# Two small products in a gated attention and SwiGLU kernel: full-array matmuls replaced by 32-wide tiles of the TensorE array

## Chip, cores and metric

The kernel runs on one NeuronCore of a Trainium2 chip. The metric is device time in microseconds for one execution. The profile is of one execution; its engines are PE (TensorE, matmul), PEld (TensorE, weight loads), DVE (VectorE), ACT (ScalarE), POOL (GpSimd) and SP (SyncE, which issues the DMAs here).

## What is computed

A token block x (2048 x 512, bf16) goes through two branches, which a gate mixes. Branch A is linear attention with 32 heads of 16 features; branch B is a SwiGLU block with 1376 hidden features.

```python
g = sigmoid((x * gate_w).sum(-1, keepdims=True))
# A: H = 32 heads, Dh = 16
q, k, v = split(x @ wqkv)
phi = lambda t: where(t > 0, t + 1, exp(t)) + 1e-6
pq, pk = phi(q), phi(k)
kv = einsum("bhsd,bhse->bhde", pk, v)
z = einsum("bhsd->bhd", pk)
num = einsum("bhqd,bhde->bhqe", pq, kv)
den = einsum("bhqd,bhd->bhq", pq, z)[..., None] + 1e-6
a = reshape(num / den) @ wo
# B
b = (silu(x @ w1) * (x @ w3)) @ w2
out = g * a + (1 - g) * b
```

## The kernel before

The 512 features are four chunks of 128 (`KC = 4`), the tokens sixteen tiles of 128 (`NT = 16`) or four blocks of 512 (`NTB = 4`). Weights and x stay in SBUF for the whole run. The order of the work on each engine is the order of the program text (a manual schedule); a tile waits where its operands or its buffer are not ready. All DMAs are issued from SP's queue, in order.

1. *Projections.* For each token tile q and k are projected (L169), phi is applied on ACT and DVE (L182 to L187), POOL adds up pk (L201), and G = xT pk is accumulated over all tiles in banks 0 to 3 (`g_step`, L217). So kv is never formed from v: it is wvT G, taken later.
2. *The first token block of branch B, with the small products between.* `glu_step` (L264, L270) runs ten times for each token block; each time it is 4 + 4 matmuls of 128x128 against 512 columns into banks 4 to 7, a Silu on ACT (L275) and a product on DVE into hT (L276). The ten steps cover the full chunks of hidden features; the rest of 96 features goes through `rem_step` (L231), which also makes the gate. After step 2 comes `kv_step`: for each of four chunks c, four matmuls accumulate a 128x128 block (8 heads x 8 heads of 16), and DVE multiplies it by the mask `bmask`, which keeps the eight 16x16 diagonal blocks (L408). After step 4 comes `m2_step`: M2[c] = kvT[c].T @ wo[c], one matmul of 512 columns for each chunk (L417), copied out by ACT (L419) and DVE (L421) in turns. After that the denominators: POOL multiplies pq by z (`den_products`, L283), DVE sums by head and takes the reciprocal (L287 to L294), POOL scales pq by it into pqs (`den_scale`, L298), and SP issues a DMA transpose of pqs into pqT (L303).
3. *Outputs.* `out_step` multiplies pqT by M2 (L429, four matmuls) and hT by w2 (L442, eleven matmuls), ACT scales the first with the gate (L434), DVE adds the second (L446), SP stores the tile. The other three token blocks then go through `glu_step` and `out_step` in the same way, each output step carrying the denominators of a tile of the next block.

PSUM has eight banks: 4 to 7 turn over for projections and GLU steps (`mm_tile`), 0 to 3 hold G and later turn over for kv, M2 and the outputs (`ab_tile`).

The masks are built on POOL at the start (L73 to L78), ahead of the memsets of `hrem` (L84). In kv's blocks and in kvT the rows are features of v, the columns features of k; in M2 the rows are features of q in their natural order, since pqT's chunk c holds features 128c to 128c + 127.

Of the kernel before, what the change touches and what calls it, by code (L numbers as in the profile page):

```python
# [8 lines left out]
ACT = mybir.ActivationFunctionType  # L9
ALU = mybir.AluOpType  # L10
AX = mybir.AxisListType
FP32 = mybir.dt.float32
BF16 = mybir.dt.bfloat16
# [3 lines left out]
def kernel(  # L17
# [17 lines left out]
    nc = tc.nc  # L35
    P = nc.NUM_PARTITIONS
# [3 lines left out]
    H = 32  # L40
    Dh = D // H
    KC = D // P
# [7 lines left out]
    HPC = P // Dh  # L50
    ZP = 4
    NR = 2 * FR + 1

    x2d = A_x.flatten_outer_dims()
    out2d = out.flatten_outer_dims()
# [5 lines left out]
    consts = ctx.enter_context(tc.tile_pool(name="consts", bufs=1))  # L61
# [10 lines left out]
    bmask = consts.tile([P, HPC, Dh], BF16, name="bmask")  # L72
    nc.gpsimd.memset(bmask[:], 1.0)  # L73
    nc.gpsimd.affine_select(
        out=bmask[:], in_=bmask[:], pattern=[[-Dh, HPC], [0, Dh]], compare_op=ALU.is_ge,
# [3 lines left out]
        out=bmask[:], in_=bmask[:], pattern=[[Dh, HPC], [0, Dh]], compare_op=ALU.is_ge,  # L79
        fill=0.0, base=Dh - 1, channel_multiplier=-1,  # L80
    )
    hrem = [consts.tile([P, TPB, P], BF16, name=f"hrem{i}") for i in range(2)]
    for h in hrem:
        nc.gpsimd.memset(h[:], 0.0)  # L84
# [16 lines left out]
    wv = consts.tile([P, KC, D], BF16, name="wv")  # L101
    wo = consts.tile([P, KC, D], BF16, name="wo")
# [29 lines left out]
    with nc.allow_non_contiguous_dma(reason="gate column"):  # L132
        dq.dma_start(
            out=wr[:, :, 2 * FR : NR], in_=gate_w.rearrange("(kc d o) -> d kc o", d=P, o=1)
        )
# [11 lines left out]
    pq = consts.tile([P, NT, D], BF16, name="pq")  # L147
    pqT = consts.tile([P, KC, S], BF16, name="pqT")
    Gsb = consts.tile([P, KC, D], BF16, name="Gsb")
    kvT = consts.tile([P, KC, P], BF16, name="kvT")  # L150
    M2 = consts.tile([P, KC, D], BF16, name="M2")
    g_all = consts.tile([P, NT], FP32, name="g_all")
    omg_all = consts.tile([P, NT], FP32, name="omg_all")
# [9 lines left out]
    def ab_tile():  # L163
        turn["ab"] += 1
        return bank[(turn["ab"] - 1) % 4]
# [57 lines left out]
    def rem_step(tb):  # L223

        hr = hrem[tb % 2]
        for half in range(2):
            ps = mm_tile()[:].rearrange("p (j n) -> p j n", j=2)
            for j in range(2):
                t = tb * TPB + half * 2 + j
                for kc in range(KC):  # L230
                    nc.tensor.matmul(  # L231
                        ps[:, j, 0:NR], lhsT=xT[:, kc, t * P : (t + 1) * P],
                        rhs=wr[:, kc, 0:NR], start=(kc == 0), stop=(kc == KC - 1),
                    )
# [44 lines left out]
    rden = {}  # L279
# [16 lines left out]
    def den_scale(t):  # L296
        pqs = work.tile([P, D], BF16, tag="pqs", bufs=3, name="pqs")
        nc.gpsimd.tensor_tensor(  # L298
            out=pqs[:].rearrange("p (h d) -> p h d", d=Dh),
            in0=pq[:, t, :].rearrange("p (h d) -> p h d", d=Dh),  # L300
            in1=rden[t][:, :, None].to_broadcast([P, H, Dh]), op=ALU.mult,
        )
        dq.dma_start(out=pqT[:, :, t * P : (t + 1) * P], in_=pqs[:], transpose=True)  # L303

    def den_step(t):

        den_sums(t)
        if t + 1 < NT:
            den_products(t + 1)
        den_scale(t)  # L310
# [86 lines left out]
            nc.scalar.activation(out=Gsb[:, kc, :], in_=bank[kc][:], func=ACT.Copy)  # L397

    def kv_step():
        kv_ps = ab_tile()[:].rearrange("p (c q) -> p c q", q=P)  # L400
        for c in range(KC):
            cs = slice(c * P, (c + 1) * P)
            for kc in range(KC):
                nc.tensor.matmul(  # L404
                    kv_ps[:, c, :], lhsT=wv[:, kc, cs], rhs=Gsb[:, kc, cs],
                    start=(kc == 0), stop=(kc == KC - 1),
                )
        nc.vector.tensor_tensor(  # L408
            out=kvT[:], in0=kv_ps,
            in1=bmask[:].rearrange("p h d -> p (h d)")[:, None, :].to_broadcast([P, KC, P]),  # L410
            op=ALU.mult,
        )

    def m2_step():
        for c in range(KC):
            ps = ab_tile()
            nc.tensor.matmul(ps[:], lhsT=kvT[:, c, :], rhs=wo[:, c, :], start=True, stop=True)  # L417
            if c % 2 == 0:
                nc.scalar.activation(out=M2[:, c, :], in_=ps[:], func=ACT.Copy)  # L419
            else:  # L420
                nc.vector.tensor_copy(out=M2[:, c, :], in_=ps[:])  # L421

    def out_step(tb, tt):
        t = tb * TPB + tt
# [38 lines left out]
    for tb in range(NTB):  # L463
        for fc in range(FC):
            glu_step(tb, fc)
            if tb == 0:
                if fc in den_at:
                    den_step(den_at[fc])
                if fc == 2:
                    kv_step()  # L470
                if fc == 4:
                    m2_step()
                    z_order()
                    den_products(0)
                if fc == 7:
                    rem_step(0)
        for tt in range(TPB):
            out_step(tb, tt)
            if tb + 1 < NTB:
                if tt == 0:  # L480
                    hT[tb + 1] = work.tile([P, FC + 1, TB], BF16, tag="hT", name="hT")
                if tt == 1:
                    rem_step(tb + 1)
                den_step((tb + 1) * TPB + tt)
# [30 lines left out]
```

## Time and profile before

| | us |
|---|---|
| Median of 3 runs (179.22 to 179.92) | 179.44 |
| Span of the profiled execution | 177.9 |
| TensorE busy in it | 174.3 |
| Four GLU matmuls of 512 columns (L264 or L270), each time | 0.86 |
| kv, 16 matmuls of 128 columns (L404) | 0.89 |
| M2, 4 matmuls of 512 columns (L417) | 0.86 |
| Mask product on DVE (L408) | 0.69 |
| M2's copies: ACT each, DVE each | 0.59, 0.68 |
| pqs product on POOL (L298), each of 16 | 1.06 |

The table's step times are pieces of the chain of work that ended last: the profile follows the end of the kernel back, at each step to what released it. In the lines of groups, the form "128*128 128x512" is the weight block and the moving block; the three durations after a colon are the shortest, the median and the longest in ns. Ends of matmuls are modelled, so the recorded length of one (379 ns for 512 columns) is longer than the distance between two starts (216 ns). The granted clock of TensorE is 1.000 over the whole span.

### The profile page before, as it was taken

How to read it: one execution, taken by the hardware profiler on the slowest of the kernel's cores; microseconds unless marked ns; L12 is line 12 of the kernel's file. 1: busy time of each engine (PE TensorE's matmuls, PEld its weight loads, DVE VectorE, ACT ScalarE, POOL GpSimd, SP SyncE). 2: the span in 40 equal slices, each digit the busy share in tenths (PEclk: the TensorE clock that was granted, in tenths of full speed). 3: DMA queues.
4: the chain of work that ended last, by engine and by line, in shares of the span. 5: the costliest groups of instructions: out<-in, count | busy, mean ns of one | idle time of the engine just before them, and what ended most of it. 6: DMA issues, size and time to landing. Idle time of an engine off the chain costs nothing.

```text
span 177.9 us, 2504 instructions
## 1 busy us (share of the span) xinstructions
PE 174.3 (98%) x879; PEld 84.1 (47%) x879; DVE 101.5 (57%) x195; ACT 62.2 (35%) x113; POOL 63.5 (36%) x105
## 2 busy tenths in 40 slices
PE   8999999999999999999999999999999999999993
PEld 5444444444454464644444464444445444444453
DVE  0299798888865888666344166634325564333222
ACT  3255444544744332331333223242321223342130
POOL 5077667557301676846300044540004432000000
DMA  6978959993103025243100013520000342000001
GB/s 175 266 209 233 168 100 315 391 350 111 33 0 29 0 55 66 66 95 106 29 0 4 0 33 85 94 57 4 0 0 29 88 92 59 0 0 0 29 33 59
DMA packets 29724, 15.41 MB, mean 87 GB/s; under 512 B 21552, under 2 KB 28048, under 8 KB 29712
## 3 DMA queue, kind: packets, MB, share of 16 engines
q1 hardware_dynamic: 29440, 15.25, 35.2%
q8 instruction: 7, 0.11, 0.3%
q10 hardware_dynamic: 272, 0.01, 0.1%
q14 instruction: 5, 0.04, 0.1%
HBM read 8.56 MB, written 2.10 MB: 60 GB/s over the span
## 4 chain that ended last, share of the span: by engine, by line
PE 98%; DVE 0%; issue 0%
PE bank L442 21%; PE bank L264 19%; PE bank L270 19%; PE bank L169 16%; PE bank L429 8%; PE bank L217 8%; PE bank L231 3%; PE bank L317 2%; PE bank L323 1%; PE bank L404 1%; PE bank L417 0%; DVE o L446 0%
## 5 line engine op out<-in xcount | busy, mean ns | idle before, releaser
L276 DVE TENSOR_TENSOR hT<-bank,sg 128x512 bf16<-128x512 f32 x40 | 27.3, 682 | 32.4 <-PE bank L270 32.4
L264 PE MATMUL bank<-xT,w 128*128 128x512 bf16 x160 | 41.1, 379 | 0.0
L270 PE MATMUL bank<-xT,w 128*128 128x512 bf16 x160 | 41.1, 379 | 0.0
L442 PE MATMUL bank<-w,hT 128*128 128x512 bf16 (+3 forms) x198 | 40.7, 355 | 0.0
L275 ACT ACTIVATE sg<-bank 128x512 bf16<-128x512 f32 x40 | 23.9, 597 | 46.7 <-PE bank L264 46.7
L298 POOL TENSOR_TENSOR pqs<-pq,rden 128x512 bf16<-128x512 bf16 x16 | 16.9, 1056 | 55.7 <-issue 48.2
L169 PE MATMUL bank<-wqk,xT 128*128 128x512 bf16 x128 | 31.2, 386 | 0.0
L442 PEld LDWEIGHTS <-hT 128*128 128x128 bf16 (+1 forms) x198 | 18.5, 98 | 19.8
L446 DVE SCALAR_TENSOR_TENSOR o<-bank,omg_all,aga 128x512 bf16<-128x512 f32 (+2 forms) x18 | 12.4, 692 | 25.6 <-PE bank L442 25.5
L201 POOL TENSOR_TENSOR zacc<-zacc,pk 128x128 f32<-128x128 f32 x56 | 23.3, 446 | 10.4 <-DVE pk L187 10.4
L270 PEld LDWEIGHTS <-w 128*128 128x128 bf16 x160 | 15.7, 98 | 18.9
L264 PEld LDWEIGHTS <-w 128*128 128x128 bf16 x160 | 15.6, 98 | 18.4
L434 ACT ACTIVATE aga<-bank,g_all 128x512 f32<-128x512 f32 x16 | 11.0, 688 | 28.9 <-PE bank L429 28.9
L169 PEld LDWEIGHTS <-xT 128*128 128x128 bf16 x128 | 12.6, 99 | 15.1 <-issue 0.6
L283 POOL TENSOR_TENSOR pr<-pq,zb 128x512 f32<-128x512 bf16 x16 | 18.5, 1156 | 0.1
L217 PE MATMUL bank<-pk,xN 128*128 128x512 bf16 x64 | 16.4, 379 | 0.0
L429 PE MATMUL bank<-M,pqT 128*128 128x512 bf16 x64 | 16.4, 378 | 0.0
L182 ACT ACTIVATE eq<-bank 128x512 bf16<-128x512 f32 x16 | 9.4, 598 | 16.0 <-PE bank L169 16.0
L187 DVE SCALAR_TENSOR_TENSOR pk<-bank,emk 128x512 bf16<-128x512 f32 x16 | 11.1, 692 | 1.6
L182 ACT ACTIVATE ek<-bank 128x512 bf16<-128x512 f32 x16 | 9.5, 597 | 7.1 <-PE bank L169 7.1
L187 DVE SCALAR_TENSOR_TENSOR pq<-bank,emq 128x512 bf16<-128x512 f32 x16 | 11.1, 692 | 0.5
L287 DVE TENSOR_REDUCE den<-pr 128x32 f32<-128x512 f32 x16 | 10.8, 676 | 0.0
(48 smaller groups left out, 82.6 us busy)
## 6 DMA issues: line engine op xcount, KB each, us to landing
w<-in_B_w_dram SPq DMA_DIRECT2D x3, 1280.0 KB, 10.1
out_dram<-o SPq DMA_DIRECT2D x15, 128.0 KB, 1.9
wqk<-in_A_wqkv_dram SPq DMA_DIRECT2D x4, 256.0 KB, 3.9
xN<-in_A_x_dram SPq DMA_DIRECT2D x1, 1024.0 KB, 5.8
xN<-in_A_x_dram SPq DMA_DIRECT2D x2, 256.0 KB, 3.1
xN<-in_A_x_dram SPq DMA_DIRECT2D x1, 512.0 KB, 3.7
wv<-in_A_wqkv_dram SPq DMA_DIRECT2D x1, 512.0 KB, 11.0
wo<-in_A_wo_dram SPq DMA_DIRECT2D x1, 512.0 KB, 12.0
```

The lines of the kernel that those rows point to most:

```text
L169: nc.tensor.matmul(ps[:], lhsT=xT[:, kc, t * P : (t + 1) * P], rhs=w[:, kc, :], start=(kc == 0), stop=(kc == KC - 1),)
L182: nc.scalar.activation(out=e[:], in_=ps[:], func=ACT.Exp)
L187: nc.vector.scalar_tensor_tensor(out=dst, in0=ps[:], scalar=0.0, in1=em[:], op0=ALU.max, op1=ALU.add)
L201: nc.gpsimd.tensor_tensor(out=(zaccb if t == NT - 1 else zacc)[:, cs], in0=zacc[:, cs], in1=pk[t][:, cs], op=ALU.add,)
L217: nc.tensor.matmul(bank[kc][:], lhsT=xN[:, t, kc * P : (kc + 1) * P], rhs=pk[t][:], start=(t == 0), stop=(t == NT - 1),)
L264: nc.tensor.matmul(g_ps[:], lhsT=w1[:, kc, fs], rhs=xT[:, kc, tok], start=(kc == 0), stop=(kc == KC - 1),)
L270: nc.tensor.matmul(u_ps[:], lhsT=w3[:, kc, fs], rhs=xT[:, kc, tok], start=(kc == 0), stop=(kc == KC - 1),)
L275: nc.scalar.activation(out=sg[:], in_=g_ps[:], func=ACT.Silu)
L276: nc.vector.tensor_tensor(out=hT[tb][:, fc, :], in0=u_ps[:], in1=sg[:], op=ALU.mult)
L283: nc.gpsimd.tensor_tensor(out=pr[t][:], in0=pq[:, t, :], in1=zb[:], op=ALU.mult)
L429: nc.tensor.matmul(a_ps[:], lhsT=pqT[:, c, ts], rhs=M2[:, c, :], start=(c == 0), stop=(c == KC - 1),)
L442: nc.tensor.matmul(b_ps[:, 0:w], lhsT=hT[tb][:n, fc, tl], rhs=w2[:n, fc, cs], start=(fc == 0), stop=(fc == FC),)
```

## The change

The heads need 16x16 diagonal blocks, and two heads fit in a 32x32 block, so all of kv lies in sixteen 32x32 diagonal blocks. The change computes only these, and uses the array in parts.

*The mask.* `bm32` (128x32) is made from `bmask` by adding its four column groups, three additions on POOL.

*kv.* For each chunk c and each contraction chunk kc, four matmuls, one for each group g of 32 features: 32 columns of weights from wv against 32 columns of G, written to partitions 32g to 32g + 31. There are 64 matmuls of 32 columns in place of 16 of 128, and the result is 128 x (4 x 32).

*M2.* For each c and g one matmul with 32 rows of kvT as weights (rows 32g on, 32 columns) against the same 32 rows of wo (512 columns), written to partitions 32c on of bank g: sixteen matmuls of 512 columns, each with a row group and a column group of its own, in place of four. The four copies then run by g, after all sixteen matmuls in program order.

*pqs.* M2's rows now come in the order g, c, head, feature, so the product that writes pqs permutes its output in the same way. The number of instructions and the DMA transposes stay the same.

```diff
+    RP = 32
+    RB = P // RP
+    HPR = RP // Dh
...
+    bm32 = consts.tile([P, RP], BF16, name="bm32")
+    bm_g = bmask[:].rearrange("p (g h) d -> p g (h d)", g=RB)
+    nc.gpsimd.tensor_tensor(out=bm32[:], in0=bm_g[:, 0, :], in1=bm_g[:, 1, :], op=ALU.add)
+    for g in range(2, RB):
+        nc.gpsimd.tensor_tensor(out=bm32[:], in0=bm32[:], in1=bm_g[:, g, :], op=ALU.add)
...
-    kvT = consts.tile([P, KC, P], BF16, name="kvT")
+    kvT = consts.tile([P, KC, RP], BF16, name="kvT")
...
-            out=pqs[:].rearrange("p (h d) -> p h d", d=Dh),
-            in0=pq[:, t, :].rearrange("p (h d) -> p h d", d=Dh),
-            in1=rden[t][:, :, None].to_broadcast([P, H, Dh]), op=ALU.mult,
+            out=pqs[:].rearrange("p (g c h d) -> p c g h d", c=KC, h=HPR, d=Dh),
+            in0=pq[:, t, :].rearrange("p (c g h d) -> p c g h d", c=KC, h=HPR, d=Dh),
+            in1=rden[t][:].rearrange("p (c g h) -> p c g h", c=KC, h=HPR)[
+                :, :, :, :, None
+            ].to_broadcast([P, KC, RB, HPR, Dh]),
+            op=ALU.mult,
...
-        kv_ps = ab_tile()[:].rearrange("p (c q) -> p c q", q=P)
+        kv_ps = ab_tile()[:, 0 : KC * RP].rearrange("p (c q) -> p c q", q=RP)
         for c in range(KC):
-            cs = slice(c * P, (c + 1) * P)
             for kc in range(KC):
-                nc.tensor.matmul(
-                    kv_ps[:, c, :], lhsT=wv[:, kc, cs], rhs=Gsb[:, kc, cs],
-                    start=(kc == 0), stop=(kc == KC - 1),
-                )
+                for g in range(RB):
+                    fs = slice(c * P + g * RP, c * P + (g + 1) * RP)
+                    nc.tensor.matmul(
+                        kv_ps[g * RP : (g + 1) * RP, c, :], lhsT=wv[:, kc, fs],
+                        rhs=Gsb[:, kc, fs], start=(kc == 0), stop=(kc == KC - 1),
+                    )
         nc.vector.tensor_tensor(
             out=kvT[:], in0=kv_ps,
-            in1=bmask[:].rearrange("p h d -> p (h d)")[:, None, :].to_broadcast([P, KC, P]),
+            in1=bm32[:, None, :].to_broadcast([P, KC, RP]),
             op=ALU.mult,
         )
...
     def m2_step():
+        ps = [ab_tile() for _ in range(RB)]
         for c in range(KC):
-            ps = ab_tile()
-            nc.tensor.matmul(ps[:], lhsT=kvT[:, c, :], rhs=wo[:, c, :], start=True, stop=True)
-            if c % 2 == 0:
-                nc.scalar.activation(out=M2[:, c, :], in_=ps[:], func=ACT.Copy)
+            for g in range(RB):
+                rows = slice(g * RP, (g + 1) * RP)
+                nc.tensor.matmul(
+                    ps[g][c * RP : (c + 1) * RP, :], lhsT=kvT[rows, c, :], rhs=wo[rows, c, :],
+                    start=True, stop=True,
+                )
+        for g in range(RB):
+            if g % 2 == 0:
+                nc.scalar.activation(out=M2[:, g, :], in_=ps[g][:], func=ACT.Copy)
             else:
-                nc.vector.tensor_copy(out=M2[:, c, :], in_=ps[:])
+                nc.vector.tensor_copy(out=M2[:, g, :], in_=ps[g][:])
```

## The prediction

> **What bounds the kernel now.** I read the page from the top: busy times, then the chain that ended last, then the lines of TensorE that the change touches, then what stands near them on the other engines.
>
> ```profile
> span 177.9 us, 2504 instructions
> PE 174.3 (98%) x879; PEld 84.1 (47%) x879; DVE 101.5 (57%) x195; ACT 62.2 (35%) x113; POOL 63.5 (36%) x105
> ...
> PE 98%; DVE 0%; issue 0%
> ```
>
> TensorE is busy for 98% of the span, and the chain is TensorE's for 98% too: after the start nothing holds it up, so a nanosecond added to its stream or taken from it is one at the end. The execution's span is 177.9 us and the median of the runs is 179.44; the 1.5 us between lie around the span, and I add my difference to the median.
>
> The chain in order of time, around the two steps that change:
>
> ```profile
> 51.36 0.86 PE bank L270 x4
> 52.23 0.89 PE bank L404 x16
> 53.12 0.86 PE bank L264 x4
> ...
> 55.71 0.86 PE bank L270 x4
> 56.57 0.86 PE bank L417 x4
> 57.44 0.86 PE bank L264 x4
> ```
>
> kv (L404) takes 0.89 us for 16 matmuls of 128 columns, 55.6 ns each; M2 (L417) takes 0.86 us for 4 of 512 columns, 216 ns each. Both sit in a dense stream. Together they are 1.75 us, 1% of the span: all that this change could win is less than that, while what it may lose has no such roof.
>
> The lines by themselves show what the rates hide:
>
> ```profile
> L404 PEld LDWEIGHTS <-wv x16: 97/98/98, 51.9 to 52.8; 128*128 128x128 bf16 x16
> L404 PE MATMUL bank<-Gsb,wv x16: 219/219/219, 52.1 to 52.9; 128*128 128x128 bf16 x16
> ...
> L417 PEld LDWEIGHTS <-kvT x4: 98/98/98, 56.2 to 56.8; 128*128 128x128 bf16 x4
> L417 PE MATMUL bank<-wo,kvT x4: 379/379/379, 56.4 to 57.1; 128*128 128x512 bf16 x4
> ```
>
> Each matmul has a weight load of its own. One takes 98 ns and starts about one matmul ahead (0.2 us ahead of a 512-column neighbour). A matmul of 128 columns is recorded as 219 ns though the next starts 55.6 ns on, one of 512 as 379 against 216: some 163 ns is depth of pipeline that a dense stream hides.
>
> **The change on TensorE.** Three terms.
>
> *kv.* 16 loads and 16 matmuls become 64 loads of 32 columns and 64 matmuls of 32 columns, on four column groups. A quarter of the columns, four times the instructions: without any overlap between groups the streamed columns are the same 2048, with perfect overlap a quarter. The trace has no matmul this short. Bounds per load and matmul: the two rates above lie on a line, (216 - 55.6)/(512 - 128) = 0.418 ns a column and 2.2 ns fixed, which gives 15.6 ns at 32 columns; and the nearest measured pair, the 128-column one, needs 55.6 ns, which is also what 32 columns would need if load and issue don't shrink with the columns. Perfect overlap of four groups lies below both, at 16 x 15.6 = 0.25 us in all. I take the middle of 15.6 and 55.6, 35 ns: a load of a quarter of the columns should be shorter, but the fixed part of a load is paid 64 times and is hidden behind a matmul that is now a quarter as long. 64 x 35 = 2.24 us against 0.89: **+1.35 us** (bounds -0.64 and 64 x 55.6 - 890 = +2.67).
>
> [...]
>
> *M2.* 4 matmuls of 512 columns become 16 of 512 columns, each on a 32x32 block of the array, with 16 loads. If the blocks run side by side, the step lasts 15 starts and one stream: 15 x 35 + 216 = 0.74 us against 0.86, **-0.12 us**. Bounds: all sixteen in the time of one, 0.22 us, -0.65; starts at 55.6 ns, 1.05 us, +0.19; and, with no concurrency at all, 16 x 216 = 3.46, +2.6, which I treat as a rival.
>
> *Going from one division of the array to another.* The stream goes full array, four column groups, full array, sixteen blocks, full array: four transitions, and the trace of before has none. Each costs between nothing and the pipeline's depth of 163 ns, if the next matmul must wait for the last to leave. I take half, 80 ns: 4 x 80 = **+0.33 us** (bounds 0 and +0.65).
>
> [...]
>
> Sum: 1.35 - 0.12 + 0.33 = **+1.56 us**: 177.9 becomes 179.5 in the profile, and 179.44 becomes **181.0**.
>
> **The change elsewhere.** All of it I cost at nothing; this is the cover.
>
> *The mask product* (L408): 128 elements a row where there were 512. It takes 0.69 us; 128x192 from a bank takes 0.36 (L241), so some 0.35 us of VectorE is saved. VectorE idles about 1.1 us ahead of each hT product there, and kvT was ready at 53.9 for a use at 56.4. Nothing gained; and if kv ends 1.4 us later, kvT is still done well ahead, since the two GLU steps between move with it.
>
> *The 32-column mask*: three additions of 128x32 on POOL, each between 0.1 us (the small memsets) and 0.45 (128x128 f32, L201), 0.3 to 1.3 us together. POOL has idle time of 6.5 us just after, before the first zacc. Without it zacc would start later by as much.
>
> *The M2 copies*: still two of 0.6 us on ScalarE and two of 0.68 on VectorE. All four banks fill at nearly the same time, so the first copy starts up to 0.5 us later, and M2 is wanted at 67.2, eight microseconds after. If they pushed sg and hT of the next GLU step, TensorE would not see it before a bank is wanted again, a step on (1.73 us).
>
> *The pqs product* (L298) writes its 512 elements permuted, in runs of 32, sixteen times:
>
> ```profile
> L298 POOL TENSOR_TENSOR pqs<-pq,rden 128x512 bf16<-128x512 bf16 x16 | 16.9, 1056 | 55.7 <-issue 48.2
> ...
> 56.88 0.65 POOL L388 COPY zb<-zpk 128x512 bf16<-128x512 bf16 x1 [10.03 <-DMA zpk<-zrow]
> ...
> 62.32 3.86 SPq L303 DMA_TRANSPOSE pqT<-pqs  x2
> 66.27 1.22 SPq L254 DMA_TRANSPOSE hT<-hrem  x1
> ```
>
> A permuted operand is seen in zb: 0.65 us for 512 elements read with a step, 0.61 for zacc's plain cast of 512 (L197). So +0.03 us or nothing an instruction; the upper bound, a doubling, is a rival below. The transposes that follow read pqs as before: the same bytes and issues, and SP's queue is moved past nothing.
>
> **The rivals.**
>
> *A, the tiles overlap as meant.* Starts at 15.6 ns: kv 64 x 15.6 = 1.0 us (+0.11), M2 15 x 15.6 + 216 = 0.45 (-0.41), transitions 0 to +0.65: between -0.3 and +0.35, so **179.1 to 179.8**, which can't be told from no change. For it: the straight line through the two rates, and that loads and matmuls overlap now. Against: that line was measured from 128 columns up. It decides as long as a pair comes in under some 27 ns in both steps, since 64 x 27 - 890 + 15 x 27 + 216 - 860 + 330 = +0.9 us: up to 180.3. [...] Chance 0.27.
>
> *B, a real gain*: kv overlaps fourfold (0.25 us, -0.64) and M2 takes one matmul's time (-0.65) with transitions almost free: **178.2 to 178.5**. It needs every bound at its best. Chance 0.05.
>
> *C, short pairs cost as much as long ones.* The supply of instructions, not the array, sets the pace: kv +2.67, M2 +0.19, transitions +0.65, sum +3.5, **182.9**. For it: 128 instructions come where 32 did, and the burst of 16 pairs at 55.6 ns may have been queued ahead during the 216 ns matmuls before it, so it proves no lasting rate. Chance 0.19. [...]
>
> *D, the blocks don't run together*, so the change doesn't do what it says: M2 3.46 us (+2.6), kv +2.67, transitions +0.65: **185.4**. Nothing in the trace speaks for serial blocks but that it shows no two matmuls on one array. Chance 0.07 with what lies between C and D.
>
> *E, POOL becomes late.* At three times its 1.06 us the first pqs ends at 64.4 in place of 62.3, the next pr product (1.16) at 65.6, the second pqs at 68.8. SP serves in order: that tile's transpose issues until 70.0, and the hT transpose behind it goes from 66.3 to 70.1 and lands 2.4 us later, at 72.5. The last of the eleven matmuls of the first output tile wants it at 68.27 + 10 x 0.216 = 70.4: 2.1 us of stall, **181.5** from this alone. At twice its time the same sum gives 70.3 and no stall, so it decides from about there, and a later TensorE adds slack. Against it stands zb's row. Chance 0.02.
>
> **How the numbers follow.** Forecast (+0.9 to +2.4 us) 0.40, A 0.27, B 0.05, C 0.19, D 0.07, E 0.02. About 0.5%, 0.9 us, is what a measurement of this kernel can tell from no change. Faster is B, 0.05; same is A, 0.27; slower is the rest, 0.68. The likeliest is the forecast, 181.0. The range leaves out B, D and the best edge of A: 179.1 to 183.6, its top being C with 0.7 us on it for the transitions' loads (a load of 98 ns that can't be hidden, four times 0.1, and as much again for M2's).
>
> **What would show it.** The chain's piece for kv: 64 matmuls in 2.2 us means 35 ns a pair; 1.0 is A, 3.6 is C. M2's piece of 0.7 us from first start to the next GLU step; 0.3 is B, 3.5 is D. Gaps of TensorE at the four borders of up to 0.16 us. pqs at 1.06 to 1.1 us, kvT near 0.3, no new wait of TensorE on POOL, VectorE or DMA. The prediction is wrong if kv's piece is under 1.5 us or over 3.3, or if TensorE stands still anywhere else.

## The result: 178.53 us, a little faster

The changed kernel takes 178.53 us (median of 19 runs, 178.17 to 179.16) against 179.23 us for the kernel before in the same comparison. The ratio is 0.9961, 95% interval 0.9951 to 0.9971: 0.70 us less, with 0.52 to 0.88 by the interval. The forecast was 181.0 us, range 179.1 to 183.6; the time lies below the range and on the other side of no change. (The forecast adds its difference to 179.44, the median of the three runs known then; over all 19 runs the kernel before takes 0.2 us less.)

The page of the changed kernel, busy times and the chain:

```profile
span 177.4 us, 2610 instructions
PE 172.9 (97%) x922; PEld 83.5 (47%) x939; DVE 101.0 (57%) x195; ACT 62.1 (35%) x113; POOL 64.2 (36%) x108
...
PE 97%; issue 1%; DVE 0%
```

TensorE is still the bound. (The matmul count is 922 where the loads are 939: some matmul records are missing, and the chain shows such holes as 0.05 us of "issue".) The chain in order of time around the two steps, in us from the start of the span, then length:

```profile
51.42 0.86 PE bank L278 x4
52.28 0.59 PE bank L416 x64
52.87 0.32 PE bank L272
...
55.57 0.86 PE bank L278 x4
56.43 0.36 PE bank L431 x16
56.80 0.97 PE bank L272 x4
```

L416 is kv, L431 M2, L272 and L278 the gate and up matmuls. kv's piece is 0.59 us where it was 0.89, M2's 0.36 where it was 0.86. What follows each is longer: the first full matmul after a step takes 0.32 in place of 0.22, and the four after M2 take 0.97 in place of 0.86. Both have to be counted, and the starts of the matmuls do that best. From the last full matmul before a step to the second or third one after it, less 216 ns for each full matmul in between and the first, kv takes **0.70 us** (0.89 before) and M2 **0.47 us** (0.86 before): -0.20 and -0.39.

The rest of the trace is as forecast: the mask product is short, pqs isn't slower, and TensorE waits for nobody. The views are of the tiles kvT and pqs:

```profile
L420 DVE TENSOR_TENSOR kvT<-bank,bm x1: 280/280/280, 53.0 to 53.0; 128x128 bf16<-128x128 f32 x1
...
L306 POOL TENSOR_TENSOR pqs<-pq,rden x16: 1055/1056/1060, 60.7 to 146.5; 128x512 bf16<-128x512 bf16 x16
```

The starts of single matmuls, from the trace's records, show where the time went (ns from one start to the next; "full" is a 512-column matmul on the whole array):

```
kv   full to first 309 | 3 4 3 28 | 5 2 4 15 | 4 2 4 15 ...
     behind the 33rd: 8 9 8 8 11 8 9 8 8 ...        last to full 116
M2   full to first 309 | 3 4 3 3 4 3 3 4 3 3 ...    last to full 317, then 226
```

In kv four matmuls start within some 10 ns, and after the first four each next four come 25 ns later; behind the 33rd there is one every 8.3 ns. M2's sixteen all start within 50 ns. A full matmul holds the next one off for 216 ns, so 309 means 93 ns lost on the way into the tiles. Theory T, put to the test below: the tiles of a step do overlap, and each step that leaves the full array costs some 0.2 us for leaving and coming back.

### The profile page after: what moved, and what is told of

Its sections match the earlier page's. It is cut to its first block, busy times and chain, and to the rows that moved or that the text cites. A ratio compares the mean times of both kernels' runs of the same rounds, so it can differ in the third digit from the quotient of the medians.

```text
span 177.4 us, 2610 instructions
## 1 busy us (share of the span) xinstructions
PE 172.9 (97%) x922; PEld 83.5 (47%) x939; DVE 101.0 (57%) x195; ACT 62.1 (35%) x113; POOL 64.2 (36%) x108
## 4 chain that ended last, share of the span: by engine, by line
PE 97%; issue 1%; DVE 0%
PE bank L460 21%; PE bank L278 20%; PE bank L272 19%; PE bank L177 16%; PE bank L225 8%; PE bank L447 8%; PE bank L239 3%; PE bank L328 2%; PE bank L334 1%; PE bank L416 0%; PE bank L431 0%; DVE o L464 0%
## 5 line engine op out<-in xcount | busy, mean ns | idle before, releaser
L278 PE MATMUL bank<-xT,w 128*128 128x512 bf16 x158 | 40.8, 379 | 0.2
L272 PE MATMUL bank<-xT,w 128*128 128x512 bf16 x156 | 40.5, 379 | 0.2
L278 PEld LDWEIGHTS <-w 128*128 128x128 bf16 x160 | 15.6, 98 | 18.9
L272 PEld LDWEIGHTS <-w 128*128 128x128 bf16 x160 | 15.5, 98 | 18.5 <-issue 0.2
```

The costliest lines, as they stand in the source:

```text
L272: nc.tensor.matmul(g_ps[:], lhsT=w1[:, kc, fs], rhs=xT[:, kc, tok], start=(kc == 0), stop=(kc == KC - 1),)
L278: nc.tensor.matmul(u_ps[:], lhsT=w3[:, kc, fs], rhs=xT[:, kc, tok], start=(kc == 0), stop=(kc == KC - 1),)
```

## The experiments

**Each half alone.** m2_alone keeps the new M2 and the old kv matmuls; kv's mask product then takes the diagonal blocks in four small products. kv_alone keeps the new kv and the old M2, with kvT zeroed at the start.

```diff
 # m2_alone: kv_step's product, after the old 16 matmuls
...
+        for g in range(RB):
+            rows = slice(g * RP, (g + 1) * RP)
+            nc.vector.tensor_tensor(out=kvT[rows, :, :], in0=kv_ps[rows, :, rows],
+                in1=bm32[rows, None, :].to_broadcast([RP, KC, RP]), op=ALU.mult)
 # kv_alone: the same, from the new 64 matmuls into a zeroed kvT of 128 columns a chunk
...
+                out=kvT[rows, :, rows], in0=kv_ps[rows, :, :],
...
```

Expected of m2_alone:

> Theory T (from the two traces): the tiles of a step overlap, and each step that leaves the full array costs some 0.09 us going in and 0.11 coming out. M2 alone then keeps its gain of 0.39 us: the step takes 0.47 us between full-array matmuls against 0.86, and kv stays at 0.89; the ratio to before is about 0.9978. Rival R3: the gain comes from other parts (kv's product on VectorE, the smaller kvT), and M2 alone gives nothing: 1.000.

Expected of kv_alone:

> T: kv alone gains 0.20 us (0.70 us between full-array matmuls against 0.89), M2 stays at 0.86; ratio to before about 0.999, and the gains of kv_alone and m2_alone add up to the change's 0.6 to 0.7 us. R3: all of the rest of the gain, some 0.3 us, is here or in neither. The record's term of +1.35 us would give 1.0075.

Measured: m2_alone 178.83 us, ratio 0.9962 (0.9949 to 0.9976); kv_alone 179.34 us, ratio 0.9989 (0.9976 to 1.0003). kv_alone's interval includes no change, so its gain rests on the trace. The steps in the traces keep their lengths. The chain of m2_alone:

```profile
51.75 0.89 PE bank L415 x16
...
56.10 0.36 PE bank L431 x16
56.46 0.97 PE bank L272 x4
```

From the last full matmul before kv to the last matmul of the kernel it is 123.06 us before, 122.67 in m2_alone (-0.39), 122.87 in kv_alone (-0.19) and 122.47 in the changed kernel (-0.59): the halves add up. By the runs' times m2_alone won more, 0.68 us with 0.43 to 0.92 by the interval, than the 0.39 of its step in the trace.

**Everything but the matmuls.** products_only is the kernel before with the 32-column mask on POOL and kv's product as four small ones into a zeroed kvT.

```diff
...
+            nc.vector.tensor_tensor(
+                out=kvT[rows, :, rows], in0=kv_ps[rows, :, rows],
+                in1=bm32[rows, None, :].to_broadcast([RP, KC, RP]), op=ALU.mult)
...
```

Expected:

> The kernel before with everything around the matmuls that m2_alone has: the 32-column mask on POOL and kv's product as four small ones, here into a zeroed kvT; all matmuls as before. m2_alone measured 0.68 us less than before while its step in the trace is only 0.39 us shorter. [...] Rival R3: the parts around the matmuls are worth some 0.2 to 0.3 us, 0.9985.

Measured: 179.38 us, ratio 0.9993 (0.9976 to 1.0010); kv is 0.89 and M2 0.86 in its chain, and from the last full matmul before kv to the last matmul it is 123.06 us, as in the kernel before: behind that point the parts around the matmuls are worth nothing. The interval of the runs does not shut out 0.2 us, so the small remainder of m2_alone stays open; the likeliest cause, not shown, is scatter ahead of the change. The last full matmul before kv starts at 51.85 us in the profile of before and at 51.37 in that of m2_alone, with the same matmuls up to there.

**Do the column groups overlap, or are short matmuls cheap by themselves?** kv_one_group issues the same 64 matmuls with the group outermost.

```diff
-        for c in range(KC):
-            for kc in range(KC):
-                for g in range(RB):
+        for g in range(RB):
+            for c in range(KC):
+                for kc in range(KC):
```

Expected:

> The same 64 matmuls in the order group, chunk, contraction, so that 16 in a row use one column group. T: neighbours can no longer overlap, a pair costs at least the straight line's 15.6 ns and up to the 55.6 of a 128-column pair: kv's first to last start takes 1.0 to 3.5 us in place of 0.47, the kernel is 0.5 to 3.0 us slower than the changed one. Rival R1: short pairs are cheap by themselves, at 6 to 8 ns each, with no overlap needed: 0.47 us and no difference.

Measured: 179.59 us, ratio 1.0012 (0.9998 to 1.0025), some 0.9 us over the changed kernel. Its chain:

```profile
51.75 1.46 PE bank L416 x64
53.20 0.32 PE bank L272
```

kv's piece goes from 0.59 to 1.46 us, by the order of its instructions alone. Between two starts in one group lie 25 ns, matmul after matmul, whether or not the next one adds to the same block; only where one group ends and the next begins do two streams interleave. So a load and matmul of 32 columns take 25 ns in a column group, and four groups share those 25 ns when their turns alternate: 6.25 ns a pair. R1 falls.

**What sets the 8.3 ns?** kv_thrice does kv's 64 matmuls three times over.

```diff
-        for c in range(KC):
+        for c in [c for _ in range(3) for c in range(KC)]:
```

Expected:

> kv's 64 matmuls done three times over, 192 in a row. T with a supply limit: the first 32 or so come four in 25 ns from a queue filled ahead, all later ones 8.3 ns apart, pairs 65 to 96 too: 0.2 + 160 x 8.3 = 1.5 us from first to last start, +1.1 us on the changed kernel. Rival: 8.3 ns belongs to the later chunks (columns or bank), so the 6.25 ns pattern returns at matmuls 65 and 129: 1.4 us. The record's 35 ns a pair: 6.7 us.

Measured: 179.94 us, ratio 1.0029 (1.0013 to 1.0046), +1.2 us on the changed kernel; the piece in the chain, which counts 189 of the 192 matmuls, is

```profile
52.39 1.66 PE bank L416 x189
54.05 0.97 PE bank L272 x4
```

The pattern of four in 25 ns ends after the 33rd start and never comes back: all the others are 8.3 ns apart, and 128 more pairs x 8.3 = 1.07 us is what the piece grew by (1.66 - 0.59). So 8.3 ns isn't bound to a place in the bank; it behaves like the rate at which new pairs are supplied once a stock of some 33 pairs is used up. That there is a stock is the author's reading and was not seen directly; m2_thrice, below, shows that, if there is one, it is not refilled all the time.

**Do M2's blocks run at the same time?** m2_thrice does its sixteen matmuls three times.

```diff
-        for c in range(KC):
+        for c in [c for _ in range(3) for c in range(KC)]:
             for g in range(RB):
```

Expected:

> M2's sixteen matmuls done three times over. T: sixteen blocks run at once, the next pass waits only for the stream of its own block: +2 x 216 ns, +0.43 us on the changed kernel, with starts in clusters of sixteen 216 ns apart. Rival R4, the block matmuls are spread over time and only their starts are close (the recorded ends are modelled): 2 x 16 x some part of 216 ns, up to +6.9 us.

Measured: 179.45 us, ratio 0.9999 (0.9980 to 1.0019), +0.7 us on the changed kernel with some 0.4 either way. The piece in the chain:

```profile
56.32 0.85 PE bank L431 x48
57.17 0.97 PE bank L272 x4
```

It grew by 0.49 us (0.85 - 0.36) for 32 more matmuls, where 0.43 was expected. The starts come in three clusters of sixteen, whose first members are 227 and 216 ns apart; behind the seventh of the last cluster they are 8.3 ns apart in place of 3.3, which is the rest. From the last full matmul before M2 to the last matmul of the kernel the trace is longer by the same 0.49 us (118.81 against 118.32). All sixteen blocks together take the time of one stream of 512 columns; R4 falls.

This run also bounds what can be said of the stock. Sixteen matmuls every 220 ns use a pair every 13.8 ns on average, so a stock of 33 that gained one pair every 8.3 ns all along would never run out here. But here too the weight loads pause behind the 33rd and then come 8.3 ns apart. The 34th load starts 416 ns after the first matmul of the step, which is recorded as 385 ns long; in kv_thrice it is 220 ns and 190. In both it comes some 30 ns after the recorded (modelled) end of that first matmul. So it looks as if nothing new is supplied until the step's first matmul has ended; no run was made to test this.

**What does a change of tiling cost?** kv_spread puts kv's four chunks behind the four gate matmuls of the next GLU step. full_spread does this to the kernel before, whose kv stays on the full array.

```diff
-                if fc == 2:
-                    kv_step()
...
 # glu_step of block 0, step 3: after each gate matmul kc, kv's matmuls of chunk kc
+            if between is not None:
+                between(kc)
```

Expected of kv_spread, then of full_spread:

> kv's four chunks of 16 matmuls, each behind one of the four gate matmuls of the next GLU step, so three more excursions out of the full array with nothing added. T: +3 x 0.2 = +0.6 us over the changed kernel, with a gap of about 0.1 us at each border. Rival R2: the gaps at the borders belong to the step's first load and last matmul in that place and not to the transition: 0 to +0.15 us.

> The control to kv_spread: the old kv, 16 matmuls on the full array, its four chunks spread between the gate matmuls of the next GLU step in the same way. T: no change of tiling, so 1.000 and kv's four parts of 0.22 us. Rival R2: splitting the step costs by itself, as kv_spread's +0.5 us.

Measured: kv_spread 179.32 us, ratio 0.9999 (0.9984 to 1.0014), some 0.7 us over the changed kernel; full_spread 179.47 us, ratio 1.0003 (0.9987 to 1.0020). The chain of full_spread, where a part of four matmuls costs its 0.22 us and the full matmul beside it keeps 0.22:

```profile
51.79 0.22 PE bank L409 x4
52.01 0.22 PE bank L264
52.23 0.22 PE bank L409 x4
```

and of kv_spread, where it grows to 0.32:

```profile
52.91 0.32 PE bank L272
53.23 0.21 PE bank L421 x16
53.44 0.32 PE bank L272
53.76 0.20 PE bank L421 x16
```

From one part to the next it is 526 ns there, 216 of them the full matmul: 310 ns a part, 1.24 us for all four in place of 0.70. That is +0.54 us for three more excursions, and nothing in the control.

The same price in the time of the whole kernel: tile_trips puts one matmul on a 128x32 tile ahead of each GLU step's gate, short_full the same with 128 columns of weights. The first gate matmul overwrites the result of both.

```diff
 # tile_trips, ahead of the gate matmuls
+        nc.tensor.matmul(
+            g_ps[0:RP, 0:RP], lhsT=w1[:, 0, fc * P : fc * P + RP],
+            rhs=xT[:, 0, tb * TB : tb * TB + RP], start=True, stop=True,
+        )
 # short_full, in its place
+            g_ps[:, 0:RP], lhsT=w1[:, 0, fs],
```

Expected of tile_trips, then of short_full:

> The changed kernel with one matmul of 32x32 outputs on a 128x32 tile ahead of the gate matmuls in each of the 40 GLU steps (its result is overwritten by the first of them), so 40 more excursions out of the full array with next to nothing in them. T: 0.2 us each, some 8 us more than the changed kernel, 186 to 187 us, with starts 0.3 us apart from the full matmul before to the tile and 0.1 us from the tile to the next. Rival R2, no price for a transition: 40 short matmuls at 6 to 56 ns, 0.3 to 2.2 us.

> The control: the same 40 extra matmuls of 32 columns, but with 128 columns of weights, on the full array. T: no transitions, so 40 x 16 to 56 ns, 0.6 to 2.2 us more than the changed kernel, some 6 us less than the one with tiles. R2: the same time as with tiles. It also prices a 32-column matmul in the full array, which the record put between 15.6 and 55.6 ns.

Measured: tile_trips 187.73 us, ratio 1.0464 (1.0447 to 1.0480); short_full 180.11 us, ratio 1.0036 (1.0024 to 1.0048). The chain of tile_trips at one GLU step:

```profile
89.91 0.86 PE bank L282 x4
90.78 0.12 PE bank L271
90.90 0.97 PE bank L276 x4
```

and of short_full:

```profile
90.80 0.86 PE bank L282 x4
91.66 0.02 PE bank L271
91.68 0.87 PE bank L276 x4
```

A GLU step with a tile in it is longer by 0.23 us: 93 ns more on the way in, 122 to the next full matmul, 11 more in that one. 40 x 0.226 = 9.0 us, which is what the ratios give (1.0464 - 0.9961 = 0.0503, of 179.4 us), and a little more than the 8 expected. A short matmul on the full array costs 28 ns from its start to the next, 1.1 us for 40, where the ratios give 1.3. R2 falls: an excursion costs 0.20 us for M2, 0.22 for kv, 0.226 here with its one short matmul, and 0.18 for each of the three more in kv_spread.

What these 0.2 us are made of stays open. On the full array a weight load starts some 0.2 us ahead of its matmul (L404 in the kernel before: first load at 51.85 us, first matmul at 52.06). On the way into the tiles of kv the first load starts 2 ns ahead of its matmul and 307 ns after the start of the last full one; on the way out it is 4 ns. So the price may lie in a wait for the matmuls ahead of the change of tiling, or in a load that can no longer be hidden; both are the author's guesses, and no run separates the two.

## Why the prediction was wrong

**The step that failed** is the price of a short load and matmul, "I take the middle of 15.6 and 55.6, 35 ns". Both values come from rows of matmuls that follow each other on the whole array. In kv, 64 starts fit in 0.48 us, 7.5 ns each; in M2 sixteen in 0.05 us, 3.3 each. The reason given for the middle, a load's fixed part "paid 64 times" behind too short a matmul, doesn't hold: loads to other column groups start as close together as the matmuls, 3 to 5 ns apart inside a turn of four in kv. Even without overlap the pair took 25 ns and not 35 (kv_one_group).

The terms, with what they measured once some 0.2 us an excursion is set apart:

| term | forecast, us | measured, us |
|---|---|---|
| kv, 0.48 in place of 0.89 | +1.35 | -0.41 |
| M2, 0.05 + 0.216 in place of 0.86 | -0.12 | -0.60 |
| four transitions | +0.33 | +0.42 |
| sum in the trace | +1.56 | -0.59 |

**The bounds held, the choice did not.** M2's lower bound of -0.65 is nearly what came (-0.60). kv's of -0.64 was not reached (-0.41): in its column group a pair takes 25 ns where the straight line gave 15.6, and behind the 33rd pair no more than one comes every 8.3 ns. Both lower bounds were given to B alone, with a twentieth of the chance, because B also wanted transitions almost free. Overlap in the steps and the price of the transitions are two separate questions; the result is overlap in both steps, with 0.42 us to pay for the transitions.

**The transitions** came near: 0.33 against 0.42. It is 93 ns on the way in and 101 to 122 on the way out. But the half of 163 ns was a choice that no row of the kernel before supported, so the nearness is in part luck, and what the price is made of was not shown.

**The rivals.** A named the overlap and allowed a gain, but priced kv by the straight line down to 15.6 ns on one stream, which left it at +0.11; so its best edge, 179.1, became the range's end. C, a supply of instructions as slow as long pairs, was off by a factor of seven in the rate, though the 8.3 ns a pair behave like such a limit. D, serial blocks, falls with m2_thrice; E, a late POOL, with pqs at its old 1056 ns. B's time, 178.2 to 178.5, is close to the 178.53 measured, but it holds a gain of 0.94 to 1.24 us on 179.44; the gain measured side by side is 0.70.

**What was costed at nothing** was nothing: pqs kept its 1056 ns (the row of zb had said +0.03 at most), kvT's product fell to 0.28 us off the path, and the mask's three additions of 0.24 us ran in POOL's idle time. What bounds the kernel was read rightly: both steps' changes reach the end in full, 0.59 us by the trace from the step to the last matmul.

**Smaller slips.** The straight line's fixed part is 2.1 ns, not 2.2, which changes nothing. The loads on top of the range, twice four times 0.1, are 0.8 us and not 0.7. And 0.9 us, given as what a measurement can tell from no change, was too coarse: nineteen runs of each kernel gave 0.70 us within 0.18 either way.

## What to carry to other kernels

Small matmuls on separate 32-wide tiles are priced as a group. M2's sixteen, each on a block of its own, took the stream of one (216 to 227 ns a pass in m2_thrice) and 3.3 ns a start; kv's, which come back to the same column groups, took 25 ns a turn, and 8.3 ns a pair behind the 33rd. On top came some 0.2 us for leaving the full array and coming back. So many of them belong in one place, in an order that alternates the groups; the same 64 matmuls cost 0.9 us more in the order that doesn't. Where two values lie far apart, ask which question each of them answers before taking the middle: here full overlap, 16 x 15.6 ns for all of kv, lay outside the two values that were averaged.

## What the runs showed of the hardware

- Four column groups with 32 columns each gave a start every 6.25 ns up to the 33rd pair, and every 8.3 ns after that, steadily over 158 pairs (kv_thrice).
- Sixteen 32x32 blocks start 3.3 ns apart, and a pass of sixteen matmuls of 512 columns takes 216 to 227 ns, where a single one on the full array takes 216 (m2_thrice).
- A short matmul on the full array costs 28 ns, on one column group 25 ns, and on a lone excursion to a tile 226 ns.
- The slow stretch at the start ends at different moments in different executions. In the profile of before the first projections start 0.43 us apart until 6.2 us into the span, in that of m2_alone until 5.5, and 0.22 us apart after that. The granted clock of 1.000 in the view of before does not show this stretch. What lies ahead of kv moves a span by up to half a microsecond (51.85 against 51.37 us to the last full matmul before it), as much as the effect studied, so that lengths from a common matmul to the end tell more than spans.
